# Chunk-selected attention and a gated MLP: every engine's order given as one list, k copied once out of PSUM, and the selections transposed in packed form

## The chip, the cores and the metric

The kernel runs on one core of a Trainium2 chip. The core has five engines that work side by side, each through its own instructions in order: PE (matrix multiply; weight loads are shown apart as PEld), ACT (activations and copies), DVE (vector operations), POOL (here masks, and the issue of loads) and SP (issue of stores and of DMA transposes). Matrix products land in PSUM[...]; everything else lies in SBUF. The metric is the device time of one execution in microseconds. The profile is of one execution and has a span, from the first to the last instruction, that is a little shorter than the time.

## What is computed

Attention over 4 batches of 8 heads, 768 positions, 64 channels. For each query row only 6 chunks of 32 keys count: those with the largest upper bound of the score, made from the smallest and largest key of each chunk. The result of all heads is the input of a gated MLP that mixes positions.

```python
k_min, k_max = min and max of k over each chunk of 32 positions
ub = sum_d max(q * k_min, q * k_max)              # per query and chunk
ub = where(own chunk or an earlier one, ub, -1e9)
top_chunks = argsort(ub)[..., -6:]
scores = scale * q @ k.T
mask = (chunk of j in top_chunks) & (i >= j)
attn = softmax(where(mask, scores, -1e9))
x = attn @ v                                      # heads side by side: 4 x 768 x 512

h = relu(x @ w_in)                                # 512 -> 1024
u, v = h[..., :512], h[..., 512:]
v_n = (v - mean(v)) / sqrt(var(v) + 1e-6)
v_s = w_spatial @ v_n + b_spatial                 # over positions, 768 x 768
out = (u * v_s) @ w_out                           # 512 -> 512
```

## The kernel before

Heads are taken two at a time: 16 pairs, four to a batch. The two heads of a pair lie beside each other in the 128 partitions (64 channels each). The mask of the selection is part of the score matmul: the operand `a` has 64 rows of q and 64 rows that hold, transposed, a 1 for each chunk that is not selected; the operand `kh` has 64 rows of k and 64 rows `expand` that hold -30000 for the chunk of each key. So one matmul of 128 rows gives score and mask.

```python
class Pair:
    def k_transpose(self):                  # PE, into a PSUM buffer of the ring "mlp" (3 buffers)
        self.kT = kT = ps_ml.tile([P, S], F16, tag="mlp", name="kTp")
        for t in range(NQT):                # NQT = 6 blocks of 128 positions
            nc.tensor.transpose(kT[:, t * P:(t + 1) * P], self.k[:, t], identity)

    def k_max(self):                        # DVE, reads PSUM; k_min is the same with min, negated
        nc.vector.tensor_reduce(self.kmm[:, 0, :], self.kT.rearrange("d (c ch) -> d c ch", ch=CHUNK),
                                axis=AX.X, op=Alu.max)

    def k_bounds(self):                     # two copies, ACT (POOL for pairs 2 and 3)
        for hi, (d0, d1) in enumerate(HALF):
            copy(self.km[d0:d1, :, hi], self.kmm[s0:s1])

    def k_operand(self, hi):                # DVE (ACT for pair 0), reads PSUM
        copy(self.kh[hi][d0:d1], self.kT[d0:d1])

    def q_transpose(self): ...              # PE, blocks 1 to 5
    def q_parts(self, m): ...               # rq = max(q, 0) and max(-q, 0), from PSUM
    def bounds(self):                       # PE: mask of later chunks, then 10 small matmuls
        mm(ub[:, 0:240], lhsT=sub_chunk, rhs=later, start=True, stop=False)
        ...
    def top(self, step): ...                # DVE: MAX8, 10 a pair
    def select(self): ...                   # DVE: ub < sixth largest -> beside q in qs

    def a_transpose(self, hi):
        if self.i >= 8:                     # pairs 8 to 15: one DMA transpose of q and selections
            if hi == 0:
                nc.sync.dma_start_transpose(out=self.a..., in_=self.qs...)
            return
        ...                                 # pairs 0 to 7: 6 PE transposes for each half
    def a_copy(self, hi):                   # pairs 0 to 7: PSUM -> a, ACT mostly
        ...

    def scores(self, hi, g):                # 6 PSUM banks of scores for each half, exp after each
        mm(sc[:, col:col + n], lhsT=self.kh[hi][:, t * P:(t + 1) * P], rhs=self.a[...], ...)
        nc.scalar.activation(out=self.e[hi][...], in_=sc[:, 0:width], func=Act.Exp, scale=scale)
    def triangle(self, hi): ...             # POOL: causal mask in the diagonal blocks (batch 0: on PE)
    def values(self, hi, blocks): ...       # PE: 21 matmuls of 65 columns a half
    def normalise(self, hi): ...            # DVE
    def x_transpose(self): ...              # PE and DVE (pairs 0-3, 15), else DMA transpose
```

The MLP of a batch starts when its four pairs are done and runs beside the attention of later pairs. Its matmuls, all of 512 columns, are 96 for `v`, `u` and `o` each and 144 for `s` over the four batches; ACT takes `v`, `u` and `o` out of PSUM, DVE the statistics, the normalisation and the gate.

The order is given by "beats": each step of each pair has a beat, and steps are emitted beat by beat. For PE up to beat 6 that is the order; later the framework's scheduler places each engine's instructions.

```python
at(t0 - 22, p.k_max); at(t0 - 20, p.k_min); at(t0 - 16, p.bounds); at(t0 - 12, p.select) ...
first, count = (b + 1) * HP * BEATS + 13, HP * BEATS      # beats of the MLP of batch b
...
with tc.manual_schedule(engines={mybir.EngineType.PE}):
    for beat in sorted(b for b in beats if b < 6): ...
for beat in sorted(beats): ...
```

Of the kernel before, what the change touches and what calls it, by code (L numbers as in the profile page):

```python
# [16 lines left out]
P = 128  # L17
# [29 lines left out]

@with_exitstack
def kernel(
# [12 lines left out]
    B, H, S, D = q.shape  # L62
# [4 lines left out]
    NQT = S // P  # L67
    NDO = DM // P
    KO = DH // P
    HP = H // 2  # L70
    NPAIR = B * HP
    CPT = P // CHUNK
    scale = 1.0 / math.sqrt(D)
    mm = nc.tensor.matmul

# [4 lines left out]
    ps_sc = ctx.enter_context(tc.psum_pool(name="ps_sc", bufs=3))  # L80
    ps_tr = ctx.enter_context(tc.psum_pool(name="ps_tr", bufs=1))
    ps_acc = ctx.enter_context(tc.psum_pool(name="ps_acc", bufs=1))
    ps_ml = ctx.enter_context(tc.psum_pool(name="ps_ml", bufs=3))

    def ml_tile():
        return ps_ml.tile([P, 512], F32, tag="mlp", name="mlp")
# [3 lines left out]

    BEATS = 12
    beats = defaultdict(list)

    def at(beat, fn, *args):
        beats[beat].append((fn, args))

    HALF = ((0, D), (D, 2 * D))


    NB = 4
    v_ring = [ring.tile([P, 4, NQT, D + 2], F16, name=f"vt{i}") for i in range(3)]
    qs_ring = [ring.tile([P, 2, NQT, 4, D], F16, name=f"qs{i}") for i in range(3)]
    km_ring = [ring.tile([P, 2, 2, NCH], F16, name=f"km{i}") for i in range(2)]
    kh_ring = [[ring.tile([P, S], F16, name=f"kh{i}_{hi}") for hi in range(2)] for i in range(NB)]
    identity = cp.tile([P, P], F16)
    tri = cp.tile([P, P], F16)
    sub_chunk = cp.tile([P, P], F16)
    later = cp.tile([P, (NQT - 1) * 2 * NCH], F16)  # L110
    expand = cp.tile([D, S], F16)
    eps_t = cp.tile([P, 1], F32)

    def init_identity():
        nc.vector.memset(identity, 0.0)
        nc.gpsimd.affine_select(out=identity, in_=identity, compare_op=Alu.not_equal, fill=1.0,
                                base=0, channel_multiplier=1, pattern=[[-1, P]])

    def init_ring(i):

        nc.vector.memset(qs_ring[i][:, :, :, 0:4:3, :], 0.0)

    def init_small():
        nc.vector.memset(km_ring[0], 0.0)
        nc.vector.memset(km_ring[1], 0.0)
        nc.vector.memset(eps_t, 1e-6)
        for t in v_ring:
            nc.vector.memset(t[:, :, :, D:D + 2], 1.0)

    def init_expand():  # L130

# [5 lines left out]

    def init_masks():

        nc.gpsimd.memset(later, 0.0)  # L140
        lv = later.rearrange("p (t h c) -> p t h c", h=2, c=NCH)
        nc.gpsimd.affine_select(out=lv, in_=lv, compare_op=Alu.is_ge, fill=NEG, base=CPT,
                                channel_multiplier=1, pattern=[[CPT, NQT - 1], [0, 2], [-1, NCH]])
        nc.gpsimd.memset(tri, 0.0)
        nc.gpsimd.affine_select(out=tri, in_=tri, compare_op=Alu.is_ge, fill=NEG,
                                base=0, channel_multiplier=-1, pattern=[[1, P]])

    def init_kh(i):
        for hi, (d0, d1) in enumerate(HALF):
            nc.scalar.copy(kh_ring[i][hi][d0:d1, :], expand)  # L150


    W = 2 * NCH
    xT = {}
    tiles = {}

    class Pair:
        def __init__(self, i):
            self.i = i
            self.b, self.hp = divmod(i, HP)  # L160
            self.heads = [4 * (self.hp // 2) + self.hp % 2 + 2 * hi for hi in range(2)]
            self.qs = qs_ring[i // 2 % 3][:, i % 2]
            self.kh, self.km = kh_ring[i % NB], km_ring[i % 2]
            self.e = {}

        def k_transpose(self):
            if self.i < 16:
                self.kT = kT = ps_ml.tile([P, S], F16, tag="mlp", name="kTp")
                for t in range(NQT):
                    nc.tensor.transpose(kT[:, t * P:(t + 1) * P], self.k[:, t], identity)  # L170
            else:
                self.kT = sb.tile([P, S], F16, tag="kT", name="kT", bufs=3)
                nc.sync.dma_start_transpose(out=self.kT.rearrange("d (t s) -> d t s", s=P),
                                            in_=self.k.rearrange("p t h d -> p (t h d)"))

        def k_max(self):
            self.kmm = sb.tile([P, 2, NCH], F16, tag="kmm", name="kmm")
            nc.vector.tensor_reduce(self.kmm[:, 0, :], self.kT.rearrange("d (c ch) -> d c ch", ch=CHUNK),  # L178
                                    axis=AX.X, op=Alu.max)

        def k_min(self):
            nc.vector.tensor_reduce(self.kmm[:, 1, :], self.kT.rearrange("d (c ch) -> d c ch", ch=CHUNK),  # L182
                                    axis=AX.X, op=Alu.min, negate=True)

        def k_bounds(self):
            for hi, (d0, d1) in enumerate(HALF):
                copy = nc.gpsimd.tensor_copy if 2 <= self.i < 4 else nc.scalar.copy
                s0, s1 = HALF[1 - hi]
                copy(self.km[d0:d1, :, hi], self.kmm[s0:s1])

        def k_operand(self, hi):
            d0, d1 = HALF[1 - hi]
            copy = nc.scalar.copy if self.i < 1 else nc.vector.tensor_copy
            copy(self.kh[hi][d0:d1], self.kT[d0:d1])  # L194

        def trans_tile(self):

            if self.b == 0:
                return ps_ml.tile([P, S], F16, tag="mlp", name="trm")
            return ps_tr.tile([P, S], F16, tag="tr", name="tr")  # L200

        def q_transpose(self):
            self.tr = self.trans_tile()
# [391 lines left out]
```

The softmax here doesn't subtract the row's maximum and nothing guards it: scores larger than these inputs give would overflow.

## Time and profile before

| | before |
|---|---|
| time, median of 3 runs | 208.71 us (208.42 to 208.72) |
| span of the profiled execution | 206.9 us |
| TensorE clock granted | 1.000 |
| PE busy | 187.8 us, 91%, 1922 matmuls |
| DVE busy | 154.5 us, 75%, 454 instructions |
| ACT busy | 158.1 us, 76%, 326 instructions |
| POOL busy | 80.5 us, 39% |

The page gives each engine's busy time over the span, then the span in 40 slices with tenths of busy time.

```profile
PE   0368999898899999999999999999999999999992
PEld 0266776775666665656655656565555454444440
DVE  6467979989799989899797999887647456365520
ACT  4797989899998889785989996669999830666042
POOL 7997659596992463236114111111111110000000
```

A digit of 9 is 90% or more of about 5.2 us. The last six slices are the MLP of the last batch alone: the attention is over, POOL has nothing to do and ACT and DVE little. In tables of stretches, each row is start:end, its length, and per engine the busy us with the number of instructions in brackets. In lists of groups a row is line, engine, operation, what is written and read, count, then busy us and mean ns, then the idle time just before it and what ended that.

### The profile page before, as it was taken

What the parts mean: (1) busy time and instruction counts of PE and PEld (TensorE: products, weight loads), DVE (VectorE), ACT (ScalarE), POOL (GpSimd) and SP (SyncE); (2) the same over time, 40 slices, a digit from 0 to 9 for tenths busy, and PEclk for the clock granted to TensorE, in tenths of its full rate; (3) what the DMA queues carried; (4) which work ended last, traced back from release to release, by engine and by line L of the source; (5) the groups of instructions that cost most, each with busy time, mean ns of one, the idle gap of its engine ahead of it and who ended that gap; (6) DMA issues with size and microseconds to landing.
All of it is one profiled execution on the core that took longest, in us unless ns stands there. A gap on an engine that the chain in (4) does not pass through costs nothing.

```text
span 206.9 us, 5068 instructions
## 1 busy us (share of the span) xinstructions
PE 187.8 (91%) x1922; PEld 115.1 (56%) x1922; DVE 154.5 (75%) x454; ACT 158.1 (76%) x326; POOL 80.5 (39%) x100
## 2 busy tenths in 40 slices
PE   0368999898899999999999999999999999999992
PEld 0266776775666665656655656565555454444440
DVE  6467979989799989899797999887647456365520
ACT  4797989899998889785989996669999830666042
POOL 7997659596992463236114111111111110000000
PEclk9999999999999999999999999999999999999999
DMA  5999999999999999979998926648782124540356
GB/s 38 92 118 154 140 178 158 173 177 167 177 162 162 97 119 128 135 130 147 149 278 153 180 62 57 127 88 158 181 166 65 38 29 92 187 152 3 72 128 256
DMA packets 114424, 27.27 MB, mean 132 GB/s; under 512 B 109536, under 2 KB 110816, under 8 KB 114400
## 3 DMA queue, kind: packets, MB, share of 16 engines
q0 software_dynamic: 76544, 12.20, 89.8%
q1 hardware_dynamic: 37856, 14.75, 36.4%
q8 instruction: 15, 0.25, 0.5%
q14 instruction: 9, 0.07, 0.1%
HBM read 24.38 MB, written 6.29 MB: 148 GB/s over the span
## 4 chain that ended last, share of the span: by engine, by line
PE 69%; ACT 17%; DVE 8%; issue 2%; DMA 2%; POOL 0%; DVEq 0%; ACTq 0%; POOLq 0%
PE mlp L388 40%; PE sc L266 12%; ACT e L271 10%; PE acc L289 7%; PE kTp L170 2%; ACT a L257 2%; DVE kmm L178 2%; PE ub L222 2%; DMA k<-in_k_dram 2%; PE trm L251 2%; ACT vraw L398 1%; PE tr L205 1%; DVE vn L412 1%; DVE kmm L182 1%; ACT u L420 1%
## 5 line engine op out<-in xcount | busy, mean ns | idle before, releaser
L271 ACT ACTIVATE e<-sc 128x512 f16<-128x512 f32 x192 | 96.9, 553 | 14.8 <-PE sc L266 13.4
L266 PE MATMUL sc<-a,kh 128*128 128x512 f16 (+3 forms) x256 | 65.5, 308 | 2.1 <-ACT e L271 1.5
L388 PE MATMUL mlp<-w_in_sb,xT 128*128 128x512 f16 x192 | 53.0, 379 | 0.1
L278 POOL TENSOR_SCALAR_AFFINE_SELECT e<-e 128x768 f16<-128x768 f16 x24 | 20.9, 869 | 66.3 <-ACT e L271 66.3
L289 PEld LDWEIGHTS <-e 128*128 128x128 f16 x672 | 31.4, 97 | 17.0 <-DVE x L297 3.8
L388 PE MATMUL mlp<-vn,wsT 128*128 128x512 f16 x144 | 37.3, 379 | 0.0
L289 PE MATMUL acc<-vt,e 128*128 128x65 f16 x672 | 35.3, 193 | 0.7 <-DVE x L297 0.4
L266 PEld LDWEIGHTS <-kh 128*128 128x128 f16 x256 | 22.7, 98 | 13.3 <-issue 0.8
L437 ACT COPY o<-mlp 128x512 f32<-128x512 f32 x24 | 14.1, 586 | 19.5 <-PE mlp L388 19.1
L400 DVE BATCH_NORM_STATS2 stats<-vraw 128x6 f32<-128x512 f32 x24 | 16.6, 693 | 12.9 <-ACT vraw L398 12.5
L388 PE MATMUL mlp<-w_out_sb,gT 128*128 128x512 f16 x96 | 25.1, 379 | 0.0
L388 PEld LDWEIGHTS <-xT 128*128 128x128 f16 x192 | 17.2, 97 | 12.6 <-issue 0.4
L427 DVE SCALAR_TENSOR_TENSOR g<-mlp,b_col,u 128x512 f16<-128x512 f32 x24 | 17.9, 748 | 7.3 <-PE mlp L388 6.2
L232 DVE MAX8 max<-ub 128x8 f32<-128x8 f32 (+4 forms) x160 | 15.6, 165 | 5.1 <-PE ub L222 4.9
L388 PEld LDWEIGHTS <-wsT 128*128 128x128 f16 x144 | 12.9, 98 | 10.4
L178 DVE TENSOR_REDUCE kmm<-kTp 128x24 f16<-128x768 f16 x16 | 15.2, 948 | 3.7 <-PE kTp L170 2.7
L297 DVE TENSOR_TENSOR x<-acc,rec 128x384 f16<-128x384 f32 x32 | 17.6, 551 | 0.4
L336 POOL DMA_DIRECT2D qs<-in_q_dram x14 | 14.6, 1049 | 5.9 <-PE sc L266 5.9
L194 DVE COPY kh<-kTp 64x768 f16<-64x768 f16 x30 | 16.5, 549 | 0.5
L398 ACT ACTIVATE vraw<-mlp 128x512 f32<-128x512 f32 x24 | 14.4, 601 | 3.0 <-PE mlp L388 3.0
L420 ACT ACTIVATE u<-mlp 128x512 f16<-128x512 f32 x24 | 14.3, 598 | 1.7 <-PE mlp L388 1.5
L327 POOL DMA_DIRECT2D k<-in_k_dram x14 | 14.4, 1045 | 2.5 <-PE kTp L170 1.8
(67 smaller groups left out, 230.2 us busy)
## 6 DMA issues: line engine op xcount, KB each, us to landing
out_dram<-o SPq DMA_DIRECT2D x24, 256.0 KB, 2.3
vt<-in_v_dram POOLq DMA_DIRECT2D x8, 384.0 KB, 8.8
k<-in_k_dram POOLq DMA_DIRECT2D x14, 192.0 KB, 8.1
qs<-in_q_dram POOLq DMA_DIRECT2D x14, 192.0 KB, 7.5
ws_raw<-in_moe_w_spatial_dram POOLq DMA_DIRECT2D x6, 192.0 KB, 6.9
w_in_sb<-in_moe_w_in_dram POOLq DMA_DIRECT2D x8, 128.0 KB, 6.9
w_out_sb<-in_moe_w_out_dram POOLq DMA_DIRECT2D x4, 128.0 KB, 7.9
k<-in_k_dram POOLq DMA_DIRECT2D x4, 96.0 KB, 3.4
```

What stands on the lines that cost most here:

```text
L178: nc.vector.tensor_reduce(self.kmm[:, 0, :], self.kT.rearrange("d (c ch) -> d c ch", ch=CHUNK), axis=AX.X, op=Alu.max)
L194: copy(self.kh[hi][d0:d1], self.kT[d0:d1])
L266: mm(sc[:, col:col + n], lhsT=self.kh[hi][:, t * P:(t + 1) * P], rhs=self.a[:, q0 // P:(q0 + n) // P, hi, :], start=True, stop=not diag)
L271: nc.scalar.activation(out=self.e[hi][:, g * 512:g * 512 + width], in_=sc[:, 0:width], func=Act.Exp, scale=scale)
L278: nc.gpsimd.affine_select(out=blk, in_=blk, compare_op=Alu.is_ge, fill=0.0, base=0, channel_multiplier=-1, pattern=[[0, NQT], [1, P]])
L289: mm(self.av[:, qi, :], lhsT=self.e[hi][:, c:c + P], rhs=self.v[hi][:, t, 0:D + 1], start=first and n == 0, stop=last and n == len(blocks) ...
L297: nc.vector.tensor_tensor(self.x16[:, :, hi, :], in0=self.av[:, :, 0:D], in1=rec.to_broadcast([P, NQT, D]), op=Alu.mult)
L388: mm(st[group][:, 0:cols], lhsT=lhsT, rhs=rhs, start=(j == 0), stop=(j == n - 1))
L398: nc.scalar.activation(st["vraw"][:, ti, :], h, func=Act.Relu)
L400: nc.vector.bn_stats(stats, st["vraw"][:, ti, :])
L420: nc.scalar.activation(st["u"][:, ti, :], h, func=Act.Relu)
L427: nc.vector.scalar_tensor_tensor(g, in0=vs, scalar=b_col[:, ti:ti + 1], in1=st["u"][:, ti, :], op0=Alu.add, op1=Alu.mult)
```

## The change

It has five parts.

1. **One list for all engines.** A long string names every step in the order in which it is emitted (`ORDER`, 1378 names), and all engines keep that order. The list came out of a small list scheduler with costs for each step, which the file carries along (only its table of engines is used when the kernel is built). Rings of k, q and v have 4 buffers instead of 3. The MLP of a batch may start at 8 beats behind its last pair instead of 13.
2. **k copied once** (pairs 2 to 15): kT is copied from PSUM to SBUF, and the bounds and operands are made from the copy; a bound is two halvings and a reduction of what is left.
3. **Bounds with one multiply** instead of two copies, and the mask of later chunks in 4 columns a block instead of 24.
4. **Packed selections** (pairs 8 to 15): q is transposed once, six blocks, and copied half by half into `a`; the selections, 24 of 32 columns for two heads and two blocks at a time, are transposed in three blocks and copied in four copies of 32 partitions. The DMA transpose of `a` is gone.
5. **The head.** k of pairs 0 and 1 and q of pair 0 are transposed twice into different banks, so that two engines can read them at once, and pair 0's selection and operand are made in parts, so that scores start from the first part.

```diff
+PLAN = {'late': 40, 'mlp_first': 8, 'qbuf': 4, 'kbuf': 4, 'vbuf': 4, 'kcp': 2, 'ca': 8}
+ORDER = """
+id0 small id1 ring0 lk000 expand lk010 ring3 kh00 lq000 ring2 kh01 lq010 ring1 kh10 mkz lk001 kh11 lk011 kT0 kh21
+... (pair 4 and the first MLP matmuls of batch 0:)
+sc415 av402 wsp4 ac50 v00.0 nm40 lq40 v01.0 ex414 kmax7 ub6 ex415 v00.2 lq41 top60 sc500 sc501 va00 top61 v01.2 tri41
+... (pair 15 and after:)
+tri151 nm150 gd21 s23.0 s22.4 av1510 gt22 s23.2 av1511 s23.4 gd22 s24.0 gt23 av1512 s24.2 nm151 s25.0 gd23 s24.4 xp15
+... """
 ...
+        def k_bound(self, m):
+            src = self.kT.rearrange("d (c ch) -> d c ch", ch=CHUNK)
+            if f"kc{self.i}" in engine or self.i >= prm["kdma"]:
+                for n in (16, 8):
+                    half = sb.tile([P, NCH, n], F16, tag=f"half{n}", name=f"half{n}")
+                    nc.vector.tensor_tensor(half, in0=src[:, :, 0:n], in1=src[:, :, n:2 * n], op=op)
+                    src = half
+            nc.vector.tensor_reduce(self.kmm[:, m, :], src, axis=AX.X, op=op, negate=(m == 1))
+        def k_copy(self, engine):
+            kT = sb.tile([P, S], F16, tag="kT", name="kT", bufs=3)
+            copier(engine)(kT, self.kT)
+            self.kT = kT
         def k_bounds(self):
-            for hi, (d0, d1) in enumerate(HALF):
-                copy(self.km[d0:d1, :, hi], self.kmm[s0:s1])
+            nc.vector.tensor_tensor(self.km, in0=self.kmm.unsqueeze(2).to_broadcast(shape),
+                                    in1=own_head.unsqueeze(1).unsqueeze(3).to_broadcast(shape), op=Alu.mult)
 ...
-            mm(ub[:, 0:(NQT - 1) * W], lhsT=sub_chunk, rhs=later, start=True, stop=False)
+            own = bass.AP(ub.tensor, ub.offset + CPT, [list(ub.ap[0]), [W + CPT, NQT - 1], [NCH, 2], [1, CPT]])
+            mm(own, lhsT=sub_chunk, rhs=later, start=True, stop=False, skip_group_check=True)
 ...
+        def q_half(self, engine, hi):                       # ACT, 64 partitions x 768
+            copier(engine)(self.a[d0:d1, :, hi, :], self.tr[d0:d1].rearrange("d (t s) -> d t s", s=P))
+        def select_packed(self): ...                        # DVE: ub < sixth largest -> mk
+        def m_transpose(self):                              # PE, three blocks
+            for j in range(NQT // 2):
+                nc.tensor.transpose(self.mt[:, j * P:(j + 1) * P], self.mk[:, j]..., identity)
+        def m_part(self, engine, hi, par):                  # DVE, 32 partitions x 384
+            src = self.mt[64 * par + 32 * hi:64 * par + 32 * hi + 32]
+            copier(engine)(self.a[d0:d0 + 32, par::2, hi, :], src.rearrange("d (t s) -> d t s", s=P))
         def a_transpose(self, hi):
-            if self.i >= 8:
-                if hi == 0:
-                    nc.sync.dma_start_transpose(out=self.a..., in_=self.qs...)
-                return
 ...
-    with tc.manual_schedule(engines={mybir.EngineType.PE}):
-        for beat in sorted(b for b in beats if b < 6): ...
-    for beat in sorted(beats): ...
+    with tc.manual_schedule():
+        for name in ORDER.split():
+            acts[name]()
```

## The prediction

> **What bounds the kernel now.** I read the table of stretches first, because the page's shares average over stages with different limits.
>
> ```profile
> core 0: us, PE busy (x) PEld busy (x) DVE busy (x) ACT busy (x) POOL busy (x), PEclk, DMA share, GB/s
> 0.00:14.00 14.00, 3.97 (x37) 3.12 (x38) 7.57 (x28) 10.01 (x14) 12.81 (x21) 1.00 1.17 75
> 14.00:30.00 16.00, 14.88 (x203) 11.27 (x201) 13.14 (x42) 13.57 (x29) 11.65 (x15) 1.00 2.75 156
> 30.00:45.00 15.00, 13.57 (x199) 10.08 (x196) 14.36 (x47) 14.01 (x31) 11.81 (x17) 1.00 1.87 170
> 45.00:60.00 15.00, 13.38 (x200) 9.63 (x198) 13.16 (x45) 14.27 (x32) 13.13 (x17) 1.00 2.12 168
> 60.00:75.00 15.00, 14.45 (x182) 9.72 (x180) 14.00 (x41) 13.08 (x29) 7.82 (x8) 1.00 1.70 127
> 75.00:150.00 75.00, 74.93 (x790) 45.40 (x787) 65.40 (x202) 62.55 (x136) 19.84 (x21) 1.00 1.25 141
> 172.00:207.00 35.00, 31.01 (x144) 13.86 (x142) 14.83 (x28) 14.57 (x26) 0.00 (x0) 1.00 0.44 129
> ```
>
> PE looks busy everywhere, but a matmul's record (379 ns for 512 columns) overlaps the next one's. So I ask how much work PE had, from pitches. The chain of waits gives the pitch: 146 matmuls of 512 columns in 31.53 us are 216 ns each.
>
> ```profile
> 22.87 3.23 ACT e L271 x8
> 26.15 1.09 ACT e L271 x2
> ...
> 171.50 31.53 PE mlp L388 x146
> 203.05 0.58 ACT o L437
> ```
>
> The other pitches I read from merged stretches of the order of time: 56 ns for 128 columns (ten transposes in 0.73 us less the last one's 0.22), 31 ns for the values product (21 in 0.81 less 0.19), 25 ns for a bounds matmul (10 in 0.41), and by columns 109 ns for 256 and 163 ns for 384. With the counts of the list of groups by shape the whole program holds: MLP 432 x 0.216 = 93.3; scores 32 halves x 1.14 = 36.5; triangle 48 x 0.056 = 2.7; values 672 x 0.031 = 20.8; transposes 338 x 0.056 = 18.9; bounds 16 x 0.10 + 160 x 0.025 = 5.6. Sum **177.8 us of PE work** in a span of 206.9.
>
> The same sum by stretch (the edges counted twice) shows where the other 29 us lie: 12.1 us of work in 14 to 30, 11.7 in 30 to 45, 12.5 in 45 to 60, 14.0 in 60 to 75, then 75.0 in 75 to 150 and 31.1 in the last 35. So the first score comes at 14.35 with some 2.4 us of PE work done (12 us lost), 14 to 75 loses **about 11 us**, the end after the last matmul is 3.9 us, and from 75 on PE has no hole worth the name. The time before 55.1, where the first MLP matmul starts, is set by ACT and DVE: 36.7 and 35.7 of 40.8 us busy, in a chain that runs through exps, reductions and copies.
>
> [...] the first score matmuls here took 634 ns against 379, so the first microseconds of scores stay slow in either kernel. [...] the SBUF copy and the two-tensor form in 16 bits are in no row here.
>
> ```profile
> L178 DVE TENSOR_REDUCE kmm<-kTp 128x24 f16<-128x768 f16 x16 | 15.2, 948 | 3.7 <-PE kTp L170 2.7 <-ACT e L271 0.7
> L194 DVE COPY kh<-kTp 64x768 f16<-64x768 f16 x30 | 16.5, 549 | 0.5
> L257 ACT COPY a<-tr 128x768 f16<-128x768 f16 x8 | 6.4, 805 | 0.0
> L189 ACT COPY km<-kmm 64x48 f16<-64x48 f16 x28 | 6.4, 229 | 0.6
> ```
>
> **Part 1: k copied once** (pairs 2 to 15). Removed per pair on DVE: two reductions and two operand copies from PSUM. I take a DVE pitch as the record less 0.07: 2 x 0.88 + 2 x 0.47 = 2.70. Added: one copy from PSUM 0.47; per bound two halvings and a reduction of 192[...], 0.74; two operand copies from SBUF[...]. Sum 0.47 + 1.48 + 0.56 = 2.51. It saves 0.2 per pair: nearly nothing. Its use is that the PSUM buffer of the "mlp" ring is free after 0.5 us instead of after four operations.
>
> **Part 2: bounds.** Two ACT copies (0.46 per pair) become one DVE multiply of 96 elements (estimated 0.18). The mask matmul shrinks from 240 to 40 columns: 16 x 0.08 = 1.3 us of PE saved.
>
> **Part 3: packed selections** (pairs 8 to 15). Gone: 8 DMA transposes (median 4.7 us to landing). They lie in 78 to 148, where PE was full, so the wait was hidden. Added per pair: on PE 1 + 3 transposes (0.22), on ACT two copies (as long as the 0.70 pitch of the existing 768-element copy), on DVE four copies of 384 elements[...]. In all +1.8 us PE, +11 us ACT, +9 us DVE. ACT had 62.6 of 75 busy there, DVE 65.4, with a pair each 10 us: ACT gains 1.4 - 0.46, DVE 1.1 + 0.18 - 0.2 per pair. DVE goes to some 97% by records, about 90% by pitch. **It brings no time, and is the main risk.**
>
> **Part 4: the head.** For pair 0, k and q are transposed twice, so that ACT and DVE read different banks, and scores start from a first third of the selection. Loads arrive as before (k at 5.6, q at 8.4). The bounds matmuls end near 11.1 as now. Then six maxima (0.5), a selection of three blocks (0.3), four cold transposes (0.6) and a copy of 512 (0.4): first score at about 13.1 instead of 14.35, **-1.2**. The doubled transposes (17 x 0.056) lie in idle time.
>
> **Part 5: the order.** Every engine gets a fixed list, the MLP may start 5 beats earlier, rings of k, q and v have four buffers. I summed the pitches along the new list. Total PE work is 177.8 - 1.3 + 1.8 + 1.0 = 179.3. From the first score to the first MLP matmul it holds PE 29.8, ACT 32.0, DVE 34.5 us; behind that PE 147, ACT 110, DVE 113. So DVE bounds the first part and PE the rest. Before, the first part took 40.8 us for much the same DVE work (87% filled). If the list fills DVE to 94%, it takes 36.7 and the MLP starts at 49.8. With 147 us of PE work and 1.5 us of holes the last matmul ends at 198.3; the end of 3.9 gives a span of 202.2. The time is 1.8 above the span now (208.71 to 206.9), so about 204.0. The filling is my choice; the bound with none lost is 13.1 + 34.5 + 147 + 3.9 + 1.8 = 200.3. As a schedule by search should lie a little nearer the bound, I say **203.5**.
>
> **Rivals.** (a) The list packs no better: at the 87% of now, and with the 3.4 us that PE lost behind 55.1 (55.1 + 144.5 of work, against 203.05), it is 13.1 + 39.5 + 147 + 3.4 + 5.7 = 208.7, the same. For it: ACT and DVE wait on each other through short chains here, which no order removes, and DMA is at 156 to 170 GB/s until 60, so w_in may land late. Against it: several waits up to 75 are of order and buffers (kT for its PSUM buffer, DVE for the x transposes 1.8 us). (b) DVE becomes the bound in pairs 8 to 15 and a static PE list stalls behind it: at 5% lost over 100 us, +5, to 208 or 210. For it: 90% by pitch, and dependent halvings each wait for the one before. Against it: the list carries MLP work between. (c) DMA transposes had cost more than seen, and all packs: 200 to 201.
>
> **Range and chances.** From the bound of 200.3 less a margin for my estimates, 199.5, to rivals (a) and (b), 208.5. Over 2% needs 204.5; my sum is just under it: 0.58 faster, 0.32 within 2%, 0.10 slower.
>
> **What would show it.** First score at 13 to 13.5; first MLP matmul at 48 to 51 against 55.1; PE pitch unchanged; no hole of PE over 0.5 us after 75; the two bounds at 0.75 us each; the extra copies of ACT and DVE beside full PE. Wrong if PE waits for DVE copies of selections (rival b), if the MLP starts at 53 or later (a), or if PE loses over 4 us after its first MLP matmul.

## The result and the profile after

| | before | after |
|---|---|---|
| time, median | 208.58 us (208.42 to 208.72) | 219.04 us (218.00 to 219.41) |
| ratio of the times | | 1.0491, 95% interval 1.0466 to 1.0516 |
| span of the profiled execution | 206.9 us | 217.0 us |
| first score matmul | 14.35 us | 13.2 us |
| first MLP matmul | 55.1 us | 51.3 us |
| PE work by pitch | 177.7 us | 179.1 us |
| PE lost behind the first MLP matmul | 2.5 us | 14.3 us |
| last exponential | 167.4 us | 178.1 us |

A pitch is the time from the start of one instruction to the start of the next one. "PE lost" is the time from each matmul's start to the next one's, less the pitch of its columns, summed. From the first MLP matmul on, the two spans compare as follows: it comes 3.8 us earlier, the work behind it is 1.7 us longer, the holes 11.8 us longer, the end 0.3 us longer. That sums to 10.0 us; the spans differ by 10.1, the rest is rounding.

The slices of the page after show that PE falls behind in its middle, where it was all nines before, and that DVE stays at sevens to nines to the end of the attention, where it had gone down to sevens and fours.

```profile
PE   0698899889898999499999798999799999999992
DVE  7597989889889888488979998988878746446520
```

The same as a table of stretches, in which the columns are as before:

```profile
75.00:150.00 75.00, 68.36 (x706) 40.38 (x704) 62.81 (x211) 57.65 (x114) 20.06 (x21) 0.98 1.10 114
150.00:182.00 32.00, 30.68 (x294) 17.50 (x293) 23.54 (x73) 25.57 (x55) 5.46 (x6) 1.00 0.29 77
182.00:217.00 35.00, 30.76 (x147) 13.81 (x144) 15.10 (x28) 13.55 (x26) 0.00 (x0) 1.00 0.43 127
```

The last 35 us are as before (30.8 of PE, 31.0 then). From 75 us to the end of the attention DVE does 86.4 us (62.81 + 23.54) where it did 77.4 before. The chain that ended last gives the same turn: before, PE had 69% of it and DVE 8%.

```profile
PE 45%; DVE 35%; DMA 8%; POOL 5%; issue 3%; ACT 2%; ACTq 0%; DVEq 0%; POOLq 0%
```

The first scores of the pairs say where. The pair that opens at 77.0 before (the eighth, pair 7) opens at 74.9 after, so the head and the first half brought 2 us. Pair 8, the first packed one, opens at 91.2 against 87.1, and from pair 9 on (98.7, against 96.7) pairs are 11.8 us apart, against 10.1. So 10.1 us are lost in the six steps from pair 9 to pair 15, by their pace and not by one hole. In these pairs PE and DVE wait for each other, from 95 to 165 us as follows (total, times, longest):

```profile
PE trq L671 <- DVE a L721: 3.0, 5, 1.2
PE acc L785 <- DVE x L793: 1.0, 1, 1.0
DVE rq L680 <- PE trq L671: 3.0, 5, 0.6
DVE max L701 <- PE ub L691: 1.4, 2, 0.8
```

The transposes of the next q (`trq`) wait until DVE has copied the selections out, and then DVE waits for these transposes. Before, from 85 to 155 us, the same view shows no wait of PE's matmuls. DVE is not full in this: from 98.7 to 169.5 us it is busy for 61.4 of 70.8, 87%.

DVE's pieces, from the list of groups by shape (count, busy us, mean ns):

```profile
L721 DVE COPY a<-trm 32x384 f16<-32x384 f16 x32 | 11.3, 353 | 1.7 <-PE trm L716 1.1
L648 DVE TENSOR_REDUCE kmm<-half 128x24 f16<-128x192 f16 x28 | 9.9, 353 | 1.0
L646 DVE TENSOR_TENSOR half<-kT 128x384 f16<-128x384 f16 x28 | 9.8, 351 | 0.2
L646 DVE TENSOR_TENSOR half<-half 128x192 f16<-128x192 f16 x28 | 8.4, 301 | 1.0
```

From start to next start in the order of time, the medians are 0.362 us for a selection copy, and 0.382, 0.293 and 0.270 for the three steps of a bound: **0.945 us a bound** in this list, where a reduction straight from PSUM has a pitch of 0.87. The operand copies of k are not DVE's: pairs 2 to 15 make them by DMA (28 transfers of 96 KB, median 5.8 us to landing). That line of the change I had overlooked, so the 0.56 us a pair that I had put on DVE for them are not there.

The largest hole of PE, at pair 8, in the order of time (start, length, engine, operation, and in brackets what it waited for):

```profile
89.60 0.75 DVE L908 SCALAR_TENSOR_TENSOR g<-mlp,b_col,u 128x512 f16<-128x512 f32 x1 [2.79 <-DMA gT<-g]
90.38 1.35 SPq L914 DMA_TRANSPOSE gT<-g  x1
90.39 1.47 DVE L721 COPY a<-trm 32x384 f16<-32x384 f16 x4
91.15 1.44 PE L759 MATMUL sc<-a,kh 128*128 128x512 f16 x3 [2.83 <-DVE a L721]
...
91.84 1.57 ACT L768 ACTIVATE e<-sc 128x512 f16<-128x512 f32 x3 [5.24 <-PE sc L759]
```

Read it upwards. ACT waited 5.2 us for scores, the scores for the copies of the selections, and the copies stood in DVE's list behind a gate. The gate waited for one of its three buffers, which a DMA transpose had not yet read. These transposes take longer to land than before, and more loads lie in the same stretch. Of 75 to 100 us, after and then before (the first line is the loads' share of the DMA engines' time, the second the median from issue to landing):

```profile
q0 software_dynamic: 19282, 2.45, 180.7%
gT<-g SPq DMA_TRANSPOSE x6, 8.3
```

```profile
q0 software_dynamic: 11532, 1.46, 133.4%
gT<-g SPq DMA_TRANSPOSE x6, 5.1
```

### The profile page after: what moved, and what is told of

Read it like the earlier page. It is cut to its first block, busy times and chain, and to the rows that moved or that the text cites. A ratio compares the mean times of both kernels' runs of the same rounds, so it can differ in the third digit from the quotient of the medians.

```text
span 217.0 us, 5264 instructions
## 1 busy us (share of the span) xinstructions
PE 192.0 (88%) x1971; PEld 117.4 (54%) x1971; DVE 166.0 (77%) x549; ACT 161.9 (75%) x316; POOL 79.4 (37%) x96
## 4 chain that ended last, share of the span: by engine, by line
PE 45%; DVE 35%; DMA 8%; POOL 5%; issue 3%; ACT 2%; ACTq 0%; DVEq 0%; POOLq 0%
PE mlp L868 27%; PE sc L759 8%; DVE half L646 7%; PE acc L785 4%; DVE a L721 4%; DVE kmm L648 4%; DMA gT<-g 4%; DVE max L701 3%; DVE x L793 3%; DMA k<-in_k_dram 3%; DVE kT L652 3%; DVE stats L891 2%; DVE vn L902 2%; DVE g L908 2%; POOL k L548 2%
## 5 line engine op out<-in xcount | busy, mean ns | idle before, releaser
L768 ACT ACTIVATE e<-sc 128x512 f16<-128x512 f32 (+1 forms) x192 | 96.4, 572 | 21.8 <-PE sc L759 18.9
L868 PE MATMUL mlp<-w_in_sb,xT 128*128 128x512 f16 x192 | 53.9, 379 | 0.1
L774 POOL TENSOR_SCALAR_AFFINE_SELECT e<-e 128x768 f16<-128x768 f16 x24 | 21.0, 876 | 87.1 <-ACT e L768 69.4
L868 PE MATMUL mlp<-vn,wsT 128*128 128x512 f16 x144 | 39.5, 382 | 0.0
L785 PEld LDWEIGHTS <-e 128*128 128x128 f16 x672 | 31.2, 97 | 13.1 <-DVE x L793 4.8
L785 PE MATMUL acc<-vt,e 128*128 128x65 f16 x672 | 36.2, 193 | 1.7 <-DVE x L793 1.7
L759 PEld LDWEIGHTS <-kh 128*128 128x128 f16 x256 | 24.2, 99 | 20.1 <-issue 4.2
L868 PE MATMUL mlp<-w_out_sb,gT 128*128 128x512 f16 x96 | 26.8, 379 | 0.0
L868 PEld LDWEIGHTS <-xT 128*128 128x128 f16 x192 | 16.5, 97 | 13.1 <-issue 0.5
L891 DVE BATCH_NORM_STATS2 stats<-vraw 128x6 f32<-128x512 f32 x24 | 16.4, 685 | 6.2 <-ACT vraw L885 6.1
L868 PEld LDWEIGHTS <-wsT 128*128 128x128 f16 x144 | 12.0, 98 | 8.7
L622 PE MATMUL kTp<-identity,k 128*128 128x128 f16 x96 | 8.6, 230 | 6.6 <-DMA k<-in_k_dram 6.6
L705 ACT COPY a<-trq 64x768 f16<-64x768 f16 x16 | 12.6, 790 | 1.3 <-DVE rq L682 0.7
```

Source lines behind the costliest of these rows:

```text
L768: nc.scalar.activation(out=self.e[hi][:, g * 512:g * 512 + width], in_=self.sc[hi, g][:, 0:width], func=Act.Exp, scale=scale)
L774: nc.gpsimd.affine_select(out=blk, in_=blk, compare_op=Alu.is_ge, fill=0.0, base=0, channel_multiplier=-1, pattern=[[0, NQT], [1, P]])
L785: mm(self.av[:, qi, :], lhsT=self.e[hi][:, c:c + P], rhs=self.v[hi][:, t, 0:D + 1], start=first and n == 0, stop=last and n == len(blocks) ...
L868: mm(st[kind, ti], lhsT=lhsT, rhs=rhs, start=(j == 0), stop=(j == n - 1))
L891: nc.vector.bn_stats(stats, st["vraw"][:, ti, :])
```

## The experiments

My theory after the result was that DVE's work sets the pace of the packed pairs. The rivals were the list itself, the late DMA landings, and the one PSUM bank "tr" through which q, the bounds and the selections pass in turn. The time of the kernel before was 208.7 to 208.9 beside all of these runs; a ratio is to it, with its 95% interval.

### Undoing parts and buffers

**e2_free**: the same names in the same order, but the scheduler may place them.

```diff
-    with tc.manual_schedule():
-        for name in ORDER.split():
-            acts[name]()
+    for name in ORDER.split():
+        acts[name]()
```

> The changed kernel with all its operations, but without the fixed order: steps are emitted in the order of the list and the framework's scheduler places each engine's instructions. (list) the holes of PE after 80 us go: 205 to 210. (packed) the chain through the one PSUM bank stays, and pairs 9 to 15 still take over 11 us each: 214 to 221. (gate) depends on where the scheduler puts the gates; 212 to 219.

218.59 us, ratio 1.0475 (1.0452 to 1.0499). Keeping the list fixed is not the cause. The scheduler was still guided by that list, so this says nothing of its content.

The trace tells more. In the list of the change the three steps of a bound stand one behind the other; here the scheduler mostly set the steps of both bounds of a pair side by side, two of each kind in a row:

```profile
117.51 0.61 DVE L646 TENSOR_TENSOR half<-kT 128x384 f16<-128x384 f16 x2
118.04 0.42 DVE L646 TENSOR_TENSOR half<-half 128x192 f16<-128x192 f16 x2
118.38 0.60 DVE L648 TENSOR_REDUCE kmm<-half 128x24 f16<-128x192 f16 x2
118.90 0.68 DVE L891 BATCH_NORM_STATS2 stats<-vraw 128x6 f32<-128x512 f32 x1
```

Two bounds in 1.39 us are 0.70 each instead of 0.945 (medians of the three steps: 0.268, 0.169, 0.262). DVE was busy for 160.3 us in all instead of 166.0, and pairs from 9 on were 11.4 us apart instead of 11.8. But the first score came at 15.4 us instead of 13.2, and two values products waited 1.9 and 2.0 us for triangles on POOL (at 52 and 71 us), so nothing was left of that gain.

**e1_dma_a**: operands of pairs 8 to 15 by DMA transpose again, all steps of packing taken from the list.

```diff
-PLAN = {..., 'ca': 8}
+PLAN = {..., 'ca': 99}      # and qa, mT, ma taken out of ORDER, aTd put behind sel
```

> The changed kernel (219.0 us, 10.4 over the one before) with the operand of pairs 8 to 15 made by one DMA transpose again, as before the change; the list is the same with the packed steps taken out. Three theories: (packed) the selection chain of pairs 8 to 15, that is 3 small transposes, 4 DVE copies and 2 ACT copies a pair, all through one PSUM bank, makes a pair 11.8 us instead of 10.1; without it the time is 204 to 208. (list) the fixed list is what fails on the chip, whatever it holds; the time stays at 214 or more. (gate) one stall of a gate behind a late DMA transpose at 82 to 91 us costs 5 to 7 us; DMA transposes in the same list do nothing against it, 212 to 219.

227.04 us, ratio 1.0868 (1.0837 to 1.0898): 8 us slower instead of faster. PE has a hole of 9.8 us at 109.6 and two smaller ones, each a score waiting for a DMA transpose. From the end of a selection to the pair's first score there are 3.9 to 6.6 us here in pairs 10 to 15, where the kernel before has 8.4 to 11.2: a list made for copies is too short for these transfers. The run doesn't tell what packing costs.

**e7_free_dma_a**: the same, placed by the scheduler.

> The changed kernel without fixed order (as in the second run, 218.6) and with the operand of pairs 8 to 15 by DMA transpose as before: what is left is the head, k copied once, the bounds and the rings. (packed) 206 to 211. (k by DMA) the transposes wait among the operand DMAs: over 213, as in the first run, where two of them held the scores for 3.3 and 9.8 us.

222.38 us, ratio 1.0650 (1.0626 to 1.0674). Again scores wait for DMA transposes (3.1 us at 94 and at 105), and one values product for a triangle on POOL (2.3 us). The scheduler still went along a list made for packing.

**e3_g6**: six gate buffers instead of three.

```diff
-tag="g", name="g", bufs=3
+tag="g", name="g", bufs=6
```

> The changed kernel with six buffers for the gate's output g instead of three, so that no gate waits for a DMA transpose to land. (gate) the hole of 3 us before pair 8, the half-speed clock behind it and what follows go: 212 to 214. (packed) the pairs from 9 on stay at 11.8 us, and only the one stall goes: 214 to 217. (list) no more than 2 us: 217 to 219.

217.41 us, ratio 1.0426 (1.0362 to 1.0490). Pair 8 opens at 88.3 instead of 91.2, later pairs stay at 11.9. The stall at pair 8 is worth about 1.6 us of time (the four runs lie at 216.3 to 219.4, so this is rough): small.

**e4_mt_ml**: the transposed selections in the MLP's ring of three PSUM banks.

```diff
-self.mt = self.trans_tile("trm")[:, 0:S // 2]
+self.mt = ps_ml.tile([P, S], F16, tag="mlp", name="trm")[:, 0:S // 2]
```

> The changed kernel with the transposed selections (pairs 8 to 15) in a buffer of the MLP's PSUM ring instead of the one bank of the q transposes and bounds. If (packed) works through that bank, PE's waits for the selection copies before the next q transposes (3.0 us in five waits) go, and the time falls by 3 to 6 us to 213 to 216. If it works through the order and load of DVE, the waits move to other instructions: 217 to 220. The MLP's ring has one buffer less for about 1.5 us a pair, which could cost 1 or 2 us.

215.95 us, ratio 1.0340 (1.0311 to 1.0368): 3 us come back. The single bank holds things up as well, but is not most of it.

### One part alone, in the old order

**e5_before_packed**: the kernel before, with the packed selections of pairs 8 to 15 put in at the old beats.

> The kernel before with the packed selections alone (pairs 8 to 15: q transposed in six blocks, two ACT copies, three transposes, four DVE copies, no DMA transpose of the operand), in the order by beats. (packed) this part alone costs most of the 10: 213 to 219. If instead the whole only suffers from the parts together, or from the operand copies by DMA, it costs little: 208 to 211.

219.90 us, ratio 1.0536 (1.0521 to 1.0551), with pairs 11.3 us apart in the mean. The holes behind 70 us are many and short (none over 0.9 us), before scores that wait for ACT's copies of q and transposes that wait for DVE's copies:

```profile
PE sc L295 <- ACT a L227: 2.5, 6, 0.6
PE tr L211 <- DVE a L281: 1.5, 3, 0.7
```

In the old order, packing alone does as much harm as the whole change.

**e6_before_kcopy**: the kernel before, with k copied once, operands by DMA.

> The kernel before with k copied once alone (pairs 2 to 15: copy to SBUF, halvings, operands by DMA from the copy), in the order by beats. (packed) this part has nothing to do with the loss: 206 to 210. (k by DMA) the 28 operand DMAs come late among the loads, 5 to 8 us each, and slow the gate's and x's DMA transposes, which waited up to 9.4 us in the changed kernel: 211 to 216.

216.54 us, ratio 1.0387 (1.0344 to 1.0430). Most comes from one hole of 4.9 us at 58, a values product that waits for its triangle on POOL, behind which PE ran at a lower granted clock (0.83 from 55 to 60 us, 0.82 from 60 to 65), and one of 1.6 us at 114, a late DMA transpose.

**e6b_before_kcopy_dve**: the same, with the operand copies on DVE.

```diff
-            copy(self.kh[hi][d0:d1], self.kT[d0:d1])       # self.kT in PSUM
+            nc.vector.tensor_copy(self.kh[hi][d0:d1], self.kT[d0:d1])   # self.kT the SBUF copy
```

> The kernel before with k copied once to SBUF in pairs 2 to 15, bounds by the halving tree from the copy, and the operand copies from SBUF on VectorE (not by DMA). Theory (VectorE's sum decides): per pair 0.475 + 2 x 0.945 + 2 x 0.37 = 3.1 us in place of 2 x 0.87 + 2 x 0.576 = 2.9, so 0.2 us more in 14 pairs and more where the copies are slow: 210 to 214, slower than before but less so than with DMA operand copies (216.5). Rival (the loss with DMA copies was VectorE's sum too, the DMA being free): at or above 216.5, as VectorE has 0.74 us more per pair than there. Rival 2 (freeing the PSUM bank early is worth something): below 208.

210.96 us, ratio 1.0100 (1.0072 to 1.0129). The time is the expected one, but the sum behind it is not borne out: in this order, too, other steps stood between those of a bound, which took 0.70 us and not the 0.945 of the sum. DVE's busy time in all is 156.1 us against 154.5 before, so copying k once saves DVE nothing here. Where the 2.1 us went was not found. Of the 7.7 us with DMA, 5.6 came with the operands' transfers and the placing that followed from them, not with the copy of k.

### DVE's work, more and less, in the new list

**e8_kop_dve**: the kernel after, with the 28 operand copies of k on DVE instead of DMA.

```diff
-kcdma=1
+kcdma=0
```

> The changed kernel, list and all, with the operands of k copied by DVE from SBUF instead of by DMA (28 copies, estimated 0.28 us each, 0.56 us of DVE a pair). (k by DMA) the landings of the gate's DMA transposes near 85 us fall from 8 us, the stall before pair 8 goes: 213 to 217. (packed, through DVE's load) DVE gets still fuller: 219 to 223.

235.35 us, ratio 1.1261 (1.1211 to 1.1311). The 28 copies have a mean of 412 ns (the 0.28 us was my estimate, and no trace had shown it); their 11.5 us cost 16.3 us of time; PE's work is unchanged. That is beyond what either theory said. In this list, work added to DVE is paid in full and more; half of it is paid before the packed pairs (the first MLP matmul comes at 59.6 us instead of 51.3).

**e10_no_ma**: the 32 selection copies left out (nothing is masked by chunk in pairs 8 to 15).

> The kernel after with all 32 copies of the transposed selections left out (the selections are still computed and transposed; the rows of the operand that would hold them are zeroed once before pairs 8 and 9, so nothing is masked by chunk in pairs 8 to 15). It is a measurement of what the copies cost. Theory (VectorE's work): 32 x 0.362 = 11.6 us less of VectorE work less 1.3 us for the two zeroings; most of it comes off the time: 208 to 211, and pairs from 9 on take 10.2 to 10.6 us each. Rival (it is the transposes, the bank's order and the late DMA landings around pair 8, not the copies): 215 to 218, pairs still 11.3 us or more.

215.22 us, ratio 1.0304 (1.0270 to 1.0337). Only 3.8 us came back of the 10.3 us of DVE work taken away, and pairs from 9 on are 11.3 us apart. My expectation of 208 to 211 was wrong, and the time is in the range of the rival: with the list kept, other waits stand in line behind the removed one (PE for ACT's q copies, 1.5 and 1.3 us; for an x transpose by DMA, 1.1 us).

**e9_ma_act**: the copies of one half (16 of 32) on ACT.

```diff
-PLAN = {'late': 40, ...}
+PLAN = {'ma_act': {(i, 1) for i in range(8, 16)}, 'late': 40, ...}
```

> The kernel after, with the two copies of each pair's transposed selections that belong to the second half (16 of the 32 copies) on ScalarE instead of VectorE, list kept. Theory (VectorE's work sets the pace of pairs 8 to 15): 2 x 0.362 = 0.72 us less of VectorE in each of eight pairs, 5.8 us in all; the time falls by 3 to 6 us, to 213 to 216, and the pairs from 9 on take about 11.2 us each in place of 11.8. Rival (the single transpose bank is what is held too long): a ScalarE copy takes longer than a VectorE one, so the bank is held as long or longer, and the time stays at 218 to 221. Rival 2 (ScalarE has no room either, its exponentials start late): over 221.

223.24 us, ratio 1.0687 (1.0652 to 1.0722): 4.2 us slower, outside both the theory and the first rival and in the range of the second. Two rows by shape show why; the last figures are the wait before and who ended it.

```profile
L671 PE MATMUL trq<-identity,qs 128*128 128x128 f16 x88 | 8.0, 229 | 6.1 <-ACT a L721 5.7 <-DVE mk L710 0.3
L721 ACT COPY a<-trm 32x384 f16<-32x384 f16 x16 | 7.5, 472 | 6.9 <-DVE a L721 6.6
```

A copy of a selection took ACT 472 ns, where it takes DVE 353. ACT's copies waited for DVE's copies out of the same bank (6.6 us in all), and PE waited 5.7 us in all for ACT's copies before the next q transposes, and 1.8 us in two waits for late exponentials. Work moved to an idle share of another engine was not free, because it was in order with two other engines there.

**e13_short_bounds**: the halvings left out, bounds from the first 8 keys of each chunk.

```diff
-                for n in (16, 8):
-                    half = ...
-                    src = half
+                src = src[:, :, 0:8]
```

> The kernel after, list kept, with the halving tree left out: the bounds of pairs 2 to 15 are reduced from the first 8 keys of each chunk (one reduction of 192 elements each, so the selection is made on a quarter of the keys). It measures what the two levels of halving cost. They take 2 x (0.382 + 0.293) = 1.35 us of VectorE per pair, 18.9 us in 14 pairs. Theory (VectorE's tree is the largest mis-sized term of the list; the generator with measured durations gives 9 us less): 208 to 211, and pairs 9 to 15 about 10.5 to 10.9 us apart. Rival (VectorE has slack behind the DMA landings and the transpose bank, so the tree is hidden): 215 or more, with pairs 11.5 us apart or more.

211.40 us, ratio 1.0131 (1.0113 to 1.0150). The 18.9 us of halvings cost 7.6 us of time, the largest single piece found, more than the selection copies. Of this 2.9 us came before the packed pairs (pair 7 opens at 72.0 instead of 74.9); from pair 9 on pairs are 11.1 us apart, between what the theory and the rival said. The largest hole left is the one at pair 8, 3.5 us.

### The list

The file carries the list scheduler that made the list. Its costs are 0.70 us for a bound, 0.29 for a selection copy, 0.59 for a normalisation and 0.68 for a half q copy on ACT; the trace has 0.945, 0.362, 0.695 and 0.82. With its own costs it sums this list to 200.7 us, with the measured ones (and DMA landings 2 to 3 us later) to 216; the chip's span is 217.0. That is arithmetic, not a measurement, but it gave the next test.

**e12_head_only**: no copy of k and no packing, rest of the change kept, placed by the scheduler along what is left of the list.

> The kernel after without the k copies and without the packed selections (bounds reduced from PSUM, operand copies of k from PSUM on VectorE, operands of pairs 8 to 15 by DMA transpose, as in the kernel before), order left to the scheduler: what is left of the change is the duplicated head, the one-multiply bounds, the 40-column mask, buffers four deep and the MLP's earlier place. Theory (the two removed parts are what costs, the rest brings what was predicted of it): first score at 13.2 to 15.5, 205 to 208. Rival (the loss lies in the new order of issue, or in the deeper prefetch that crowds the DMA queues): 211 or more, as with the kernel without packed selections alone (222).

218.53 us, ratio 1.0472 (1.0420 to 1.0523). My theory failed here: without either part it is as slow as with both. Scores wait for DMA transposes again (2.7 us at 102, 2.4 at 137). Either the rest of the change is bad, or the order is, being made for other work. The next runs tell.

**e16_relist_none**: the same work with six gate buffers, and a fixed list made anew for it from measured durations.

> The change without its two parts (no copy of k, no packed selections; operands of pairs 8 to 15 by DMA transpose as before), six gate buffers, with the list made anew for it from measured durations. The generator gives 203.5 (209.5 if DMA landings are 2.5 us later than reckoned). Theory 1 (the free order's 218.5 was a list unfit for this work): 205 to 211. Rival (a fixed or guided list cannot serve the DMA transposes, whose landing varies from 2.4 to 9 us): 214 or more.

209.45 us, ratio 1.0027 (1.0016 to 1.0038). The order was worth 9 us (the six gate buffers went with it, but in e12 no gate had waited for one). With a fitting list the head, the smaller mask and the earlier MLP together give what the kernel before gives, no more.

**e14_relist**: the kernel after, same instructions, engines and buffers, only a list made anew from measured durations. Around the first score of pair 8:

```diff
-... gt03 s04.0 kop100 av711 ma800 kop101 lq70 s04.2 ma801 gd03 av712 ma810 sc800 ma811 sc801 ...
+... ma801 s03.2 ma810 av702 s03.4 lk71 ma811 nm70 kT10 qT9 sc714 kc10 sc715 ... sc800 kop100 sc801 gt03 ...
```

In the list of the change the gate `gt03` stands ahead of the copies `ma8..`, and these right before `sc800`; in the new one the copies come first, and well ahead.

> The kernel after with the same instructions, buffers and engines, only the list made anew: the kernel's own generator with the durations that the trace shows (bound by the tree 0.945, selection copy 0.362, bound multiply 0.237, normalisation 0.69, half q copy 0.82, and slower DMA landings), and a random search over its priorities. Theory 1 (the order was made from wrong durations): the generator gives 204 where it gives 216 for the present list; with the same offset of about 1 to 3 us, 206 to 209 in time. Theory 2 (the work of VectorE does not fit, whatever the order): 215 or more.

213.70 us, ratio 1.0227 (1.0204 to 1.0250): 5.3 us better with the same work, between the ranges of the two theories. PE's longest waits from 75 to 175 us are now for a DMA transpose that landed 8.6 us after its issue and for a gate, not for the selections:

```profile
PE mlp L868 <- DMA xT<-x: 2.0, 1, 2.0
PE mlp L868 <- DVE g L908: 0.8, 1, 0.8
```

**e15_relist_best**: list made anew, with six gate buffers, the selections in the MLP's banks, and each bound one reduction of the SBUF copy.

> The list made anew with measured durations and three changes: six gate buffers in place of three, the transposed selections in the MLP's PSUM buffers, and the bounds of pairs 2 to 15 as direct reductions from the SBUF copy of k (reckoned at 0.87 us each) in place of the halving tree. The generator gives 202; theory 1: 204 to 207, faster than the kernel before by 1 to 2%. Theory 2: 212 or more.

210.23 us, ratio 1.0054 (1.0028 to 1.0081). The best kernel with both parts of the change, and still not better than before.

### The sound parts in the old order

**e17_mask**: the kernel before with the mask in 40 columns, nothing else.

```diff
-            mm(ub[:, 0:(NQT - 1) * W], lhsT=sub_chunk, rhs=later, start=True, stop=False)
+            mm(own, lhsT=sub_chunk, rhs=later, start=True, stop=False, skip_group_check=True)
```

> The kernel before with one thing of the change: the mask of later chunks written as a matmul of 40 columns in place of 240, in the old order. Theory (PE without holes after 75 us is the limit there): 16 x (102.5 - 25 ns) = 1.2 us less PE work by pitch, of which the pairs after 75 us (some 9 of 16 and all work behind them) get 0.7 to 1.2 us: 207.4 to 208.1. Rival (the old list depends on PE's pace, shorter work only moves the wait): within 0.3 us of 208.7.

211.20 us, ratio 1.0091 (1.0072 to 1.0109): less work of PE by 1.2 us, and about 2 us slower, which neither the theory nor the rival had. The largest new hole is at 56 us, where a values product waits 1.7 us for its triangle. In POOL's order of time the load of v (L345) has come ahead of the triangle (L280):

```profile
53.83 1.42 POOL L345 DMA_DIRECT2D vt<-in_v_dram  x1 [1.33 <-PE trm L312]
55.30 0.87 POOL L280 TENSOR_SCALAR_AFFINE_SELECT e<-e 128x768 f16<-128x768 f16 x1
```

In the kernel before, the triangle went first (L278; L343 is the load):

```profile
52.93 0.86 POOL L278 TENSOR_SCALAR_AFFINE_SELECT e<-e 128x768 f16<-128x768 f16 x1
53.74 1.43 POOL L343 DMA_DIRECT2D vt<-in_v_dram  x1
```

**e18_mask_mlp8**: the same with the MLP from beat 8 instead of 13.

```diff
-        first, count = (b + 1) * HP * BEATS + 13, HP * BEATS
+        first, count = (b + 1) * HP * BEATS + 8, HP * BEATS
```

> The same with the MLP's matmuls given places from beat 8 instead of beat 13 of the next batch. Theory (PE's holes before 75 us can be filled by MLP work that comes earlier): the first MLP matmul at about 52 in place of 55.1, 1 to 2 us fewer holes between 50 and 75: 205.5 to 207.5. Rival (earlier MLP work brings its VectorE and ScalarE steps earlier too, in the stretch in which these set the pace, and holds attention back): 208.5 or more.

217.53 us, ratio 1.0385 (1.0339 to 1.0432), in the range of the rival, but not in its way. The first MLP matmul came at 53.7 (57.2 in e17), but the holes from 50 to 75 us did not shrink, and the next batch's MLP came before its input:

```profile
98.04 1.34 SPq L307 DMA_TRANSPOSE xT<-x  x1
...
106.77 0.39 PE L390 MATMUL mlp<-w_in_sb,xT 128*128 128x512 f16 x1 [4.58 <-DMA xT<-x]
```

The transpose took 8.7 us to land, and for the 4.58 us before that matmul PE ran nothing else; ACT then waited 4.8 us for its product. Here the earlier place for filler work was a loss, because its input was not there yet.

## Why the prediction was wrong

It gave 203.5 us and 199.5 to 208.5; the time is 219.0.

**Right:** the head (first score 13.1 predicted, though the terms given for it add up to 12.9; measured 13.2), PE's total work (179.3 predicted, 179.1), the end nearly unchanged, and packing as the main risk. In the head two engines did read side by side: before, ACT's first copy of k waited 0.98 us for DVE's reductions out of the same buffer; after, with two buffers, ACT's copies ran from 7.77 to 9.37 us beside DVE's reductions (6.61 to 8.43). The first matmuls are slow in both kernels, as I had expected from the 634 ns before: up to 16.4 us transposes mostly start 0.107 us apart (0.056 later; the "cold" ones of Part 4), and the first score matmuls of 512 columns take 634 ns before and 584 to 622 after (379 later), while the granted clock is shown as 1.00. That k copied once, with operand copies on DVE, saves DVE next to nothing is borne out by e6b. The first MLP matmul came at 51.3, between the 49.8 of the sum and the 53 of rival (a).

**The step that failed is Part 5's last sum:** "With 147 us of PE work and 1.5 us of holes". The work there is 147.0; the holes are 14.3. The sign that I had named for it, over 4 us lost, is the one that came. The sum took PE as the bound behind the first MLP matmul because DVE had only 113 us of work there by pitch. By its busy time DVE had 122.9, so that total was not far off, and still 24 us below PE's. The step compared totals over 150 us. But PE and DVE wait for each other within the packed pairs, and a total says nothing of that. Rival (b), a list that stalls behind DVE in pairs 8 to 15, was near the right mechanism, and its 5% was too little: pairs went from 10.1 to 11.8 us, 17%. Not that the list is static (e2_free has 11.4 us a pair without it), nor that DVE is full (it is busy for 87%).

**Under it, terms of Parts 1 and 3 were mis-sized.** A bound was reckoned at 0.74 and has 0.945 in this list; a selection copy at 0.28 and has 0.362. The reckoned figures, like the 0.18 for the bound multiply (0.25 in this list) and the 0.28 for an operand copy, were my estimates: no row of the trace before shows these operations. I took a pitch as the record less 0.07, and the records that came (medians of 347, 258 and 353 ns for the three steps of a bound, 352 for a selection copy) give 0.75 and 0.28 by that. So what failed is the overlap: a halving is followed at once by the step that reads it, and then the pitch is the record plus some 0.035 (0.382 and 0.293), and the selection copies did not overlap either (0.362). In e2_free, where other steps lie between, the bound has 0.70: there the 0.74 would have been right.

For a packed pair that is 0.41 + 0.33 = 0.74 us more of DVE than I had, but the 0.56 us of operand copies had gone to DMA, so only some 0.2 us is left. And e2_free, in which DVE's busy time is 5.7 us shorter, still has 11.4 us a pair, 1.3 more than before. So these sizes are at most a smaller part of the loss.

**"It brings no time"** (Part 3) was too kind: alone, packing costs 11 us in the old order.

**Where the 10 us come from**, as far as runs show it. Order: 219.0 to 213.7, 5.3 us, came back with a list made anew from measured durations. How much of this is due to the durations, and how much to a new search, was not separated; the gate ahead of the copies is its clearest case, and six gate buffers alone brought about 1.6. Work: with lists made anew, the change costs 213.7 and its version without the two parts 209.45. That is 4.3 us for k copied once and packing, of which 1.8 is PE's work (179.1 against 177.4). It is the most that can be put down to the work, because the two differ in gate buffers too, and e15, which has both parts, six gate buffers, another bank for the selections and plain reductions, is only 0.8 us above the version without. The rest, 0.7 us, is what the other parts fail to bring in a fitting list.

**Not settled.** My theory that DVE's work alone sets the pace of the packed pairs is not borne out: taking 10.3 and 18.9 us of it away brought 3.8 and 7.6 (e10, e13), moving 5.8 us of it to ACT cost 4.2 (e9). Which of the waits between PE, ACT and DVE makes the rest was not separated. In the old order all five changes that I tried cost 2 to 11 us, even less work for PE. The kernel before loses less than 1 us from 80 to 170, so its order is a good one, which each of these changes disturbed; whether a better order exists for either kernel I can't say. The random search behind the new lists may be far from the best, and its sums (some 204, 202 and 203.5 us for e14, e15 and e16) lie 8.6, 6.9 and 3.6 us below the spans of the profiles; in the first two the longest holes are matmuls waiting for DMA transposes (2.2 and 1.9 us). Four buffers for k, q and v were not tried back at three alone, so the part of the deeper prefetch in the late landings is argued from the DMA's shares, not shown.

## What to carry to other kernels

A fixed list of instructions is only as good as the durations behind it: put measured pitches into it before its order is trusted. Small operations that need each other are the case to watch: one behind the other a bound took 0.945 us, with other steps between 0.70. And a list made for one set of work serves another badly: here it was 9 us wrong. Engines that hand a buffer to and fro in every round are judged by the round, not by totals: here DVE had over 30 us to spare by the sum (113 against 147) and still held PE up in the packed pairs. Filler work should stand in the list behind the latest, not the median, landing of its input: in e18 one landing of 8.7 us held PE for 4.6.

## What the runs showed of the hardware

- A copy of 768 columns from PSUM took DVE 549 ns on 64 partitions (operand copies before) and 550 on 128 (kT after): the partitions left idle saved nothing.
- On DVE a halving that reads the result of the one before starts about 35 ns after its end (0.382 us from start to start for 347 ns recorded). With a step behind it that does not need the result, the same halving has 0.268 in e2_free, so that step starts some 80 ns before the end; the product of the normalisation has 0.475 for 557 recorded. The selection copies, which do not need each other either, have 0.362 for 353.
- A halving tree of two levels for 768 elements took 0.945 us where its steps followed each other and 0.70 where others lay between; one plain reduction from PSUM took 0.87.
- The same DMA transpose of a gate took 2.4 to 9.3 us to land in the kernel after; in the quiet stretch behind 115 us the 96 KB copies of k land in 2.1 us, around 88 us in 8.3.
- After the hole of 3 us at pair 8 PE's granted clock was 0.66 from 90 to 95 us (0.50 from 92 to 94), and the score matmuls of 512 columns that came first started 0.38 to 0.43 us apart instead of 0.216: this stall cost more than its length.
